# A 384-byte pad ahead of the SBUF tiles, and weight loads whose reads take four rows at once

## The chip, the cores and the metric

The kernel runs on one core of one Trainium2 chip. The metric is the device time of one execution in microseconds (us). Only that core is given work. "Before" is the kernel as it was, "changed" is the kernel with the change.

## The reference

One decode step of an attention layer, gated by a small MLP. Only the sizes matter here: the K and V caches are 268 MB of the 279 MB that are read, and they are read once.

```python
B, Sq, D = 4, 1, 448
Hq, Hkv, Sk, Dh = 16, 8, 8192, 256        # K and V: 4*8 heads of 8192 x 256 bf16 = 4 MiB each
xn = _layernorm(x)
q = (xn @ wq)                              # wq 448 x 4096
scores = einsum(q, k) * Dh ** -0.5         # softmax over 8192 keys
s = (softmax(scores) @ v) @ wo             # wo 4096 x 448
g = _silu(_B_ref(xn, w1, w2, w3, w4))      # _B_ref at S = 1: xn + gelu(layernorm(xn) @ w3) @ w4, w3 448 x 1792, w4 1792 x 448
return x + s * g
```

## The kernel before

All large loads are issued by SP on one queue, in this order: wq, w3, w4, K head 0, K head 1, most of wo, and then in turn K head h and V head h-2. Two buffers hold K, two hold V. The MLP weights lie in the V buffers until V needs them. A partition gets one contiguous row: 32768 B of K or V, 1792 B of wo per query head, 12544 B of w3, 6272 B of w4 (twice).

```python
kn = sb("kn", [P, 2, NCH, DH], BF16)            # first tile of all: byte 16512 of a partition
vb = sb("vb", [P, 2, NCH, DH], BF16)
kT = sb("kT", [P, RING, TB * P], BF16)
wo_sb = sb("wo_sb", [P, HQ, NHALF, D], BF16)
# ... cut
def prog_sp(sp):
    # ... cut: wq -> vb[1]
    sp.dma_start(vflat[0][:, 0:DK * FH], B_w3...).then_inc(S["dw3"], 16)
    sp.dma_start(w4_sb..., B_w4...).then_inc(S["dw4"], 16)

    def load_k(h):
        b, g = where(h)
        if h >= 2:
            sp.wait_ge(S["v_k"], h - 1)          # all of head h-2 has been transposed
        sp.dma_start(kn_dst(h), A_k_cache[b, g]...).then_inc(S["dk%d" % (h % 2)], 16)
    # ... cut: load_v, which waits for v_v in the same way; the last V head comes in four pieces
    load_k(0)
    load_k(1)
    load_wo(NLATE, HQ, "dwo")                    # 12 heads of wo, the early load
    for h in range(2, NH):
        load_k(h)
        load_v(h - 2)
    load_v(NH - 2)
    load_v(NH - 1)
    for i, hs in enumerate(LATE):                # 4 heads of wo, the late load
        load_wo(hs[0], hs[-1] + 1, "dwl%d" % i)
```

PE first computes q and the MLP, then runs warm-up matmuls, then goes through the heads. DVE counts `v_k` up when a head's last group has been copied out.

```python
# PE
for i in range(NWARM):                           # NWARM = 14
    pe.matmul(psv[0:PVW, 0:QW], pT[:, 0, 0:PVW], wq_sb[:, 0, 0:QW], start=True, stop=True)
def f_t(h, j):                                   # group j of 16: transposes of K
    if j == 0:
        take(pe, "dk%d" % (h % 2), 16)
# DVE
for j in range(NGR):
    if j in D_GROUPS:
        evac(v, h, j)                            # waits for the transposes of group j
    # ... cut
v.sem_inc(S["v_k"], 1)
```

Of the kernel before, what the change touches and what calls it, by code (L numbers as in the profile page):

```python
# [1 line left out]

# [8 lines left out]
BF16 = dt.bfloat16  # L11

P = 128
# [19 lines left out]
def bass_recurrent_scan__gqa_block_cached__mixer_s_mlp__decode_kernel(  # L33
# [16 lines left out]
    HQ = HD // DH  # L50
# [3 lines left out]
    NHF = 2  # L54
    DK = D * NHF // P
    assert D * NHF == DK * P and DK % 2 == 1 and D == DK * (P // 2)
    HDH, FH = HD // NHF, F // NHF
    NFK = FH // P
# [30 lines left out]
    LATE = ((0, 1), (2,), (3,))  # L89
    NLATE = sum(len(g) for g in LATE)  # L90
    NWARM = 14
    QW = HDH // NQD
    assert QW <= 512 and QW % P == 0 and NQC == NQD * (QW // P)

# [7 lines left out]
    with ExitStack() as es:  # L102
        def sb(name, shape, dty):
            return es.enter_context(nc.sbuf_tensor(name, shape, dty))

        kn = sb("kn", [P, 2, NCH, DH], BF16)
        vb = sb("vb", [P, 2, NCH, DH], BF16)
        kT = sb("kT", [P, RING, TB * P], BF16)
        wo_sb = sb("wo_sb", [P, HQ, NHALF, D], BF16)
# [46 lines left out]
        S = {n: es.enter_context(nc.semaphore(n)) for n in (  # L156
            ["dx", "dwq", "dw3", "dw4", "dwo", "dk0", "dk1", "dv0", "dv1", "dout"]
            + ["dvl%d" % i for i in range(NPIECE)] + ["dwl%d" % i for i in range(len(LATE))]
            + ["p_td", "p_ta", "p_sc", "p_m1", "p_m2", "p_m3", "p_tr", "p_ou", "p_pv", "p_x", "p_q", "p_h", "p_h2", "p_o"]
            + ["v_ev", "a_ev", "v_rmax", "v_diag", "v_neg", "v_ot", "a_exp", "g_q", "g_c",  # L160
               "v_s", "v_a", "v_qb", "p_qt", "v_h2", "p_hs", "v_k", "v_v", "v_po", "v_o", "g_o", "g_p", "g_f", "v_xT", "v_qT", "v_hT", "v_c", "v_w", "a_c", "v_out"])}


        vflat = [vb[:, i].rearrange("p c d -> p (c d)") for i in range(2)]
        wq_sb = vflat[1][:, 0:DK * HDH].rearrange("p (j n) -> p j n", j=DK)
        w3_sb = vflat[0][:, 0:DK * FH].rearrange("p (j n) -> p j n", j=DK)
        w4_sb = vflat[0][:, DK * FH:DK * FH + NF * D].rearrange("p (a k n) -> p a k n", a=NHF,
                                                                k=NFK)
# [16 lines left out]
        def store(eng, i):  # L185
            eng.dma_start(out2d[:, i * DQ:(i + 1) * DQ], out_b[i * PQ:i * PQ + Bn, :]
                          ).then_inc(S["dout"], 16)

        def prog_sp(sp):
            sp.dma_start(vflat[1][:, 0:DK * HDH],  # L190
                         A_wq.rearrange("d (t n) -> (d t) n", t=NHF).rearrange(
                             "(p j) n -> p (j n)", j=DK)).then_inc(S["dwq"], 16)
            sp.dma_start(vflat[0][:, 0:DK * FH],
                         B_w3.rearrange("d (t n) -> (d t) n", t=NHF).rearrange(
                             "(p j) n -> p (j n)", j=DK)).then_inc(S["dw3"], 16)
            sp.dma_start(w4_sb.rearrange("p a k n -> p a (k n)"),
                         B_w4.rearrange("(a p k) n -> p a (k n)", a=NHF, k=NFK)
                         ).then_inc(S["dw4"], 16)

            def load_k(h):  # L200
                b, g = where(h)
                if h >= 2:
                    sp.wait_ge(S["v_k"], h - 1)
                sp.dma_start(kn_dst(h), A_k_cache[b, g].rearrange("(p c) d -> p (c d)", p=P)
                             ).then_inc(S["dk%d" % (h % 2)], 16)

            def load_v(h):
                b, g = where(h)
                src = A_v_cache[b, g].rearrange("(p c) d -> p c d", p=P)
                if h < NH - 1:  # L210
                    sp.wait_ge(S["v_v"], h + 1)
                    sp.dma_start(vflat[h % 2], src.rearrange("p c d -> p (c d)")
                                 ).then_inc(S["dv%d" % (h % 2)], 16)
                else:

                    sp.wait_ge(S["v_k"], h)
                    for i in range(NPIECE):
                        lo, hi = PIECES[i], PIECES[i + 1]
                        sp.dma_start(
                            kn[:, 1 - h % 2, lo:hi, :].rearrange("p c d -> p (c d)"),  # L220
                            src[:, lo:hi, :].rearrange("p c d -> p (c d)")
                        ).then_inc(S["dvl%d" % i], 16)

            load_k(0)
            load_k(1)
            wo_src = A_wo.rearrange("(h p c) n -> p h (c n)", p=P, c=NHALF)

            def load_wo(lo, hi, sem):
                sp.dma_start(wo_sb[:, lo:hi].rearrange("p h c n -> p h (c n)"),
                             wo_src[:, lo:hi]).then_inc(S[sem], 16)  # L230

            load_wo(NLATE, HQ, "dwo")
            for h in range(2, NH):
# [4 lines that stand above are left out]
            for i, hs in enumerate(LATE):  # L238
                load_wo(hs[0], hs[-1] + 1, "dwl%d" % i)
            sp.wait_ge(S["v_out"], 1)  # L240
            store(sp, 0)
            take(sp, "dout", 16 * NDG)

        def take(eng, name, n=1):
            eng.wait_ge(S[name], n).then_inc(S[name], -n)  # L245
# [285 lines left out]
        def prog_pe(pe, xn_mark, xn2_mark):  # L531
            pe.wait_ge(S["g_c"], NPI)
            for k, (src, mark) in enumerate(((xn_b, xn_mark), (xn2_b, xn2_mark))):
                pe.wait_ge(S["v_c"], mark)
                for j in range(DK):
                    ins = pe.transpose(xT_ps[:, k, j, :],  # L536
                                       src[:, j].rearrange("b m t -> b (m t)"),
                                       ident_b[0:Bn, 0:Bn])
# [5 lines left out]
            for j in range(DK):  # L544
                for i in range(NQD):
                    ins = pe.matmul(q_ps[i * PQ:i * PQ + NHF * Bn, 0:QW],
                                    xnT[:, j].rearrange("p a b -> p (a b)"),
                                    wq_sb[:, j, i * QW:(i + 1) * QW],
                                    start=(j == 0), stop=(j == DK - 1))
# [4 lines left out]
            for k in range(NFK):  # L554
                for j in range(DK):
                    ins = pe.matmul(h_ps[:, k * NHF * Bn:(k + 1) * NHF * Bn], w3v[:, j, k, :],
                                    xn2T[:, j], start=(j == 0), stop=(j == DK - 1))
# [3 lines left out]
                ins = pe.transpose(qt_ps[:, m * P:(m + 1) * P], q_b[:, m * P:(m + 1) * P],  # L561
                                   ident_b[:, :])
            ins.then_inc(S["p_qt"], 1)
            take(pe, "dw4", 16)
            take(pe, "v_hT")
            for k in range(NFK):
                for a in range(NHF):
# [94 lines left out]
            h = NH - 1  # L662
# [39 lines left out]

            def finish():
                f_bc(h)
                take(pe, "dwo", 16)
                pe.wait_ge(S["g_f"], 1)
                f_ou(range(NLATE, HQ - 3 * REP))
                take(pe, "v_po")
                f_warm(4)
                take(pe, "a_exp")  # L710
                pe.matmul(psm[:, P + REP:P + 2 * REP], ones_f[:, :], rowsum[:, h % 2, :],
                          start=True, stop=True)
                f_tr(ot_dst, REP).then_inc(S["p_m3"], 1)
                f_warm(2)
                take(pe, "dv%d" % ((h - 1) % 2), 16)
                f_pv(h - 1, 0, NCH)
                take(pe, "v_ot")
                f_ou(range(HQ - 3 * REP, HQ - 2 * REP))
                f_warm(2)
                take(pe, "v_po")  # L720
                f_tr(lambda dh: ot_dst(dh, 1), REP, 1).then_inc(S["p_tr"], 1)
                f_warm(3)
                take(pe, "dvl0", 16)
                pb = PIECES[NPIECE - ND]
                f_pv(h, 0, PIECES[1], pb, vl)
                take(pe, "v_ot")
                f_ou(range(HQ - 2 * REP, HQ - REP)).then_inc(S["p_ou"], 1)
                f_warm(3)
                for i in range(1, NPIECE - ND):
                    take(pe, "dvl%d" % i, 16)  # L730
                    f_pv(h, PIECES[i], PIECES[i + 1], pb, vl)
                take(pe, "v_a")
                for i in range(NDG):
                    pe.matmul(o_ps[i * PQ:(i + 1) * PQ, 0:DQ], selb[:, :],
                              ou_f[:, i * DQ:(i + 1) * DQ], start=True, stop=False)
                f_direct(NPIECE - ND)
                take(pe, "v_po")
                for dh in range(NHALF):
                    for i in range(CP):
                        pe.matmul(ol_ps[:, dh * PVW:(dh + 1) * PVW],  # L740
                                  po[:, 0, i * DH + dh:(i + 1) * DH:NHALF], sel[:, i, :],
                                  start=False, stop=False)
                f_direct(NPIECE - 1).then_inc(S["p_pv"], 1)
                take(pe, "dwl0", 16)
                f_o(LATE[0])
                take(pe, "v_ot")
                f_o(range(HQ - REP, HQ))
                for i in range(1, len(LATE)):
                    take(pe, "dwl%d" % i, 16)
                    ins = f_o(LATE[i], i == len(LATE) - 1)  # L750
                ins.then_inc(S["p_o"], 1)
# [61 lines left out]
```

## Time and profile before

| before | |
|---|---|
| median of 5 runs | 657.46 us (657.27 to 658.13) |
| span in the profile | 656.9 us |
| DMA rate, 60 to 620 us | 432 GB/s, mean DMA share 1.00 |
| PE busy, same stretch | 484.5 of 560 us |

The first lines are from the page of the kernel before: span, busy time of engines, the mean busy share of the 16 DMA engines in 40 slices (in tenths), the queue's packets with their share of the 16 engines' span, and DMA issues with the median us from issue to landing.

```profile
span 656.9 us, 22864 instructions
...
PE 556.3 (85%) x9937; PEld 476.3 (73%) x9937; DVE 276.5 (42%) x589; ACT 256.0 (39%) x364; POOL 13.4 (2%) x77
...
DMA  8999999999999999999999999999999999999996
...
q1 hardware_dynamic: 12328, 278.99, 99.2%
...
kn<-in_A_k_cache_dram SPq DMA_DIRECT2D x32, 4096.0 KB, 25.7
vb<-in_A_v_cache_dram SPq DMA_DIRECT2D x31, 4096.0 KB, 31.3
...
wo_sb<-in_A_wo_dram SPq DMA_DIRECT2D x1, 2688.0 KB, 44.3
```

The DMA engines are busy in all slices. PE, the busiest compute engine, stands still for 15% of the span. The table of stretches of the kernel before says the same of the middle, and shows that the stretch with the early wo load (36 to 44 us) moves fewer bytes. Its columns are the stretch, its length, busy time of each engine (with instructions), the granted PE clock, the DMA share and GB/s. The rate of a stretch of a few us is coarse, because a packet of 32 KB takes over a microsecond (1213 to 1222 ns, below).

```profile
core 0: us, PE busy (x) PEld busy (x) DVE busy (x) ACT busy (x) POOL busy (x), PEclk, DMA share, GB/s
36.00:44.00 8.00, 8.00 (x174) 7.20 (x170) 3.81 (x8) 4.12 (x5) 0.00 (x0) 1.00 0.95 361
44.00:47.00 3.00, 2.95 (x50) 1.68 (x44) 0.93 (x4) 0.00 (x0) 0.17 (x1) 1.00 1.22 480
47.00:50.00 3.00, 2.00 (x35) 1.86 (x36) 1.81 (x4) 1.41 (x2) 0.01 (x1) 1.00 0.97 415
60.00:620.00 560.00, 484.50 (x8812) 421.48 (x8810) 233.01 (x470) 223.90 (x320) 9.21 (x57) 0.89 1.00 432
```

The timeline of the end shows what follows the last data: 24 matmuls and the first of two DVE steps.

```profile
651.61 2.41 PE L687 MATMUL pst<-wo_sb,OT 128*32 128x224 bf16 x24 [0.50 <-PEq L245]
654.06 0.38 DVE L526 TENSOR_TENSOR res<-pst,sg 64x224 f32<-64x224 f32 x1 [2.61 <-PE pst L687]
```

The trace also has a record of every DMA packet (start, duration, size), from which I work out means below. K and V packets of 32768 B took 1213 to 1222 ns, mean 1217.2, between 100 and 600 us. wo rows of 1792 B took 74 ns at least and 78.4 on average in the early load.

### The profile page before, as it was taken

The numbers are of one execution on the slowest core, as the hardware profiler recorded it, in microseconds if no ns is written. First come the engines' busy times: TensorE is split into PE (matmuls) and PEld (weight loads), VectorE is DVE, ScalarE is ACT, GpSimd is POOL, SyncE is SP. The second block draws the span as 40 slices with busy tenths as digits, with TensorE's granted clock in tenths as the row PEclk, the third lists the DMA queues.
The fourth block names the chain that finished last, engine by engine and source line by source line (L and its number), as shares of the span: only waits on it lengthen the run. The fifth ranks groups of instructions, "written<-read, shape, count | busy, mean of one in ns | idle before, by whom it ended". The sixth has DMA issues, their size and how long they took to land. (4 is left out here: it accounts for less than half of the span.)

```text
span 656.9 us, 22864 instructions
## 1 busy us (share of the span) xinstructions
PE 556.3 (85%) x9937; PEld 476.3 (73%) x9937; DVE 276.5 (42%) x589; ACT 256.0 (39%) x364; POOL 13.4 (2%) x77
## 2 busy tenths in 40 slices
PE   1899997988888988888897888898888889888897
PEld 0487886876766887667787766798767678766775
DVE  7353554443443444434443443444334443433442
ACT  4144544442433443323444333444333344433340
POOL 2000000000000000000000000000000000000000
PEclk9698999887899878889987888988878987887998
DMA  8999999999999999999999999999999999999996
GB/s 360 440 413 425 434 427 437 425 439 427 437 427 435 429 435 431 431 435 427 437 429 433 429 433 429 433 429 433 429 435 431 433 431 435 429 433 433 429 425 256
DMA packets 12353, 279.13 MB, mean 425 GB/s; under 512 B 1204, under 2 KB 3256, under 8 KB 3768
## 3 DMA queue, kind: packets, MB, share of 16 engines
q1 hardware_dynamic: 12328, 278.99, 99.2%
q8 instruction: 7, 0.11, 0.1%
q14 instruction: 2, 0.02, 0.0%
q10 hardware_dynamic: 16, 0.01, 0.0%
HBM read 278.99 MB, written 0.00 MB: 425 GB/s over the span
## 5 line engine op out<-in xcount | busy, mean ns | idle before, releaser
L588 PE MATMUL pst<-ident_b,kn 128*128 128x128 bf16 x4096 | 347.3, 239 | 78.6 <-PEq L245 76.3
L295 ACT ACTIVATE kT<-pst 128x1024 bf16<-128x1024 bf16 x224 | 229.3, 1024 | 360.6 <-ACTq L245 359.5
L588 PEld LDWEIGHTS pst<-ident_b,kn 128*128 128x128 bf16 x4096 | 275.4, 108 | 84.3 <-issue 83.8
L293 DVE COPY kT<-pst 128x1024 bf16<-128x1024 bf16 x288 | 197.5, 691 | 263.7 <-DVEq L245 263.7
L600 PE MATMUL psc<-qc,kT 128*128 128x2 bf16 x4096 | 178.7, 165 | 0.0
L600 PEld LDWEIGHTS psc<-qc,kT 128*128 128x128 bf16 x4096 | 157.7, 98 | 28.5 <-issue 28.3
L639 PE MATMUL psv<-vb,pT 128*4 128x512 bf16 x1056 | 86.4, 378 | 0.3 <-issue 0.3
L618 PE MATMUL psm<-sel,po 128*128 128x2 f32 x272 | 36.8, 257 | 0.5 <-PEq L245 0.5
L618 PEld LDWEIGHTS psm<-sel,po 128*128 128x128 f32 x272 | 34.8, 197 | 0.9 <-issue 0.9
L639 PEld LDWEIGHTS psv<-vb,pT 128*4 128x4 bf16 x1056 | 22.3, 82 | 15.3 <-issue 0.8
L452 DVE TENSOR_REDUCE rmax<-psc 128x2 f32<-128x128 f32 x32 | 9.3, 292 | 48.8 <-DVEq L245 48.8
L470 DVE COPY po<-psv 128x512 f32<-128x512 f32 x34 | 23.5, 692 | 3.0 <-DVEq L245 2.3
L457 DVE TENSOR_REDUCE gmax<-psm 2x1 f32<-2x128 f32 x32 | 8.9, 279 | 34.7 <-DVEq L245 34.7
L317 ACT ACTIVATE pT<-psc,negb 128x64 bf16<-128x64 f32 x66 | 20.6, 331 | 5.4 <-ACTq L245 5.4
L612 PEld LDWEIGHTS psm<-diag,ones_f 2*128 2x128 f32 x66 | 14.1, 263 | 6.4 <-issue 5.4
L280 POOL COPY qc<-qT 128x4 bf16<-128x4 bf16 x32 | 5.9, 186 | 585.8 <-DVEq L469 568.6
L612 PE MATMUL psm<-diag,ones_f 2*128 2x2 f32 x66 | 16.8, 321 | 1.1 <-PEq L245 0.9
L317 ACT ACTIVATION_READ_ACCUMULATOR pT<-psc,negb 128x1 f32 x66 | 13.6, 206 | 0.0
L608 PEld LDWEIGHTS psm<-ident_f,rmax 128*2 128x2 f32 x32 | 2.6, 80 | 14.0 <-issue 14.0
L536 PE MATMUL pst<-ident_b,xn_b 4*128 4x4 bf16 x14 | 0.6, 161 | 13.6 <-DVE xn_b L365 8.9
L630 PE MATMUL psm<-rowsum,ones_f 128*128 128x2 f32 x64 | 11.6, 251 | 0.0
L536 PEld LDWEIGHTS pst<-ident_b,xn_b 4*128 4x128 bf16 x14 | 0.5, 100 | 13.6 <-issue 8.9
(101 smaller groups left out, 122.4 us busy)
## 6 DMA issues: line engine op xcount, KB each, us to landing
kn<-in_A_k_cache_dram SPq DMA_DIRECT2D x32, 4096.0 KB, 25.7
vb<-in_A_v_cache_dram SPq DMA_DIRECT2D x31, 4096.0 KB, 31.3
vb<-in_A_wq_dram SPq DMA_DIRECT2D x1, 3584.0 KB, 11.7
vb<-in_B_w_dram SPq DMA_DIRECT2D x2, 1568.0 KB, 16.6
wo_sb<-in_A_wo_dram SPq DMA_DIRECT2D x1, 2688.0 KB, 44.3
kn<-in_A_v_cache_dram SPq DMA_DIRECT2D x1, 2048.0 KB, 25.2
kn<-in_A_v_cache_dram SPq DMA_DIRECT2D x1, 1024.0 KB, 27.3
kn<-in_A_v_cache_dram SPq DMA_DIRECT2D x2, 512.0 KB, 28.5
```

The costliest lines, as they stand in the source:

```text
L293: engine.tensor_copy(dst, src).then_inc(S["v_ev"], 1)
L295: engine.activation(dst, src, ACT.Copy).then_inc(S["a_ev"], 1)
L317: ins = act.activation(pv_p[:, :, hh], sc[:, :, hh], ACT.Exp, bias=negb[:, s, hh:hh + 1], scale=SCALE, accum_out=rowsum[:, s, hh:hh + 1])
L452: v.tensor_reduce(rmax[:, :], psc[h % 2][:, 0:NCH * REP].rearrange("p (k h) -> p h k", h=REP), AX.X, ALU.max).then_inc(S["v_rmax"], 1)
L457: v.tensor_reduce(gmax[:, :], psm[0:REP, 0:P], AX.X, ALU.max).then_inc(S["v_s"], 1)
L470: v.tensor_copy(po[:, slot], psv[:, 0:CP * DH]).then_inc(S["v_po"], 1)
L588: ins = pe.transpose(dst[:, t * P:(t + 1) * P], kn[:, h % 2, GC * j + kl, half * P:(half + 1) * P], ident_b[:, :])
L600: ins = pe.matmul(psc[h % 2][:, kk * REP:(kk + 1) * REP], kT[:, j % RING, t * P:(t + 1) * P], qc[:, h % 2, half, :], start=(half == 0), st ...
L612: pe.matmul(psm[:, P:P + REP], ones_f[0:REP, :], diag[:, :], start=True, stop=True).then_inc(S["p_m2"], 1)
L618: ins = pe.matmul(dst(dh)[:, 0:width], po[:, slot, i * DH + dh:(i + 1) * DH:NHALF], sel[:, i, 0:width], start=(i == 0), stop=(i == CP - 1))
L630: pe.matmul(psm[:, P + REP:P + 2 * REP], ones_f[:, :], rowsum[:, h % 2, :], start=True, stop=True)
L639: ins = pe.matmul(psv[o:o + CP * REP, 0:CP * DH], pT[:, h % 2, kk * REP:(kk + CP) * REP], src[:, kk:kk + CP, :].rearrange("p c d -> p (c d)"),
```

## The change

The intent: rows that start on an aligned address in SBUF, and fewer, longer reads for the weights whose rows are short. `load_rows` builds the ordinary DMA of 128 rows and replaces its source pattern by 32 rows of four times the length. The destination stays 128 rows, one per partition. Each head of wo and each half of w4 becomes a DMA of its own, so wo takes 16 DMAs instead of 4.

```diff
+    ROW_PAD = 192
+        align = sb("align", [P, ROW_PAD], BF16)
         kn = sb("kn", [P, 2, NCH, DH], BF16)
 ...
+        def load_rows(eng, dst, src, rows, sem):
+            with nc.discard():
+                made = eng.dma_start(dst, src).ins
+            ap, = made.ins
+            n = ap.ap[0][1] * ap.ap[1][1]
 ...
+            pat = [[n // rows, rows], [1, n // rows]]
+            wide = bass.AP(ap.bass_ap.tensor, ap.bass_ap.offset, pat)
+            eng.add_instruction(copy.replace(
+                made, name=nc.get_next_instruction_name(), ant_dge_precooked=False,
+                ins=(copy.replace(ap, ap=pat, bass_ap=wide),))).then_inc(S[sem], 16)
 ...  (w3: one load_rows; w4: one load_rows for each half)
             def load_wo(lo, hi, sem):
-                sp.dma_start(wo_sb[:, lo:hi].rearrange("p h c n -> p h (c n)"),
-                             wo_src[:, lo:hi]).then_inc(S[sem], 16)
+                for hq in range(lo, hi):
+                    load_rows(sp, wo_sb[:, hq].rearrange("p c n -> p (c n)"), wo_src[:, hq],
+                              32, sem)
 ...
-            take(pe, "dw4", 16)
+            take(pe, "dw4", 16 * NHF)
-                take(pe, "dwo", 16)
+                take(pe, "dwo", 16 * (HQ - NLATE))
-                take(pe, "dwl0", 16)
+                take(pe, "dwl0", 16 * len(LATE[0]))
```

More of the change, by code (lines that the diff above doesn't have):

```diff
@@ L1 @@
+import copy
 from contextlib import ExitStack
@@ L187, in store @@
                           ).then_inc(S["dout"], 16)
+        def load_rows(eng, dst, src, rows, sem):
[3 more added lines that the diff above has]
+            n = ap.ap[0][1] * ap.ap[1][1]
+            assert len(ap.ap) == 2 and ap.ap[0] == (ap.ap[1][1], P) and ap.ap[1][0] == 1
+            assert rows % 32 == 0 and P % rows == 0
+            pat = [[n // rows, rows], [1, n // rows]]
[3 more added lines that the diff above has]
+                ins=(copy.replace(ap, ap=pat, bass_ap=wide),))).then_inc(S[sem], 16)
         def prog_sp(sp):
@@ L192, in prog_sp @@
                              "(p j) n -> p (j n)", j=DK)).then_inc(S["dwq"], 16)
-            sp.dma_start(vflat[0][:, 0:DK * FH],
-                         B_w3.rearrange("d (t n) -> (d t) n", t=NHF).rearrange(
-                             "(p j) n -> p (j n)", j=DK)).then_inc(S["dw3"], 16)
-            sp.dma_start(w4_sb.rearrange("p a k n -> p a (k n)"),
-                         B_w4.rearrange("(a p k) n -> p a (k n)", a=NHF, k=NFK)
-                         ).then_inc(S["dw4"], 16)
+            load_rows(sp, vflat[0][:, 0:DK * FH],
+                      B_w3.rearrange("d (t n) -> (d t) n", t=NHF).rearrange(
+                          "(p j) n -> p (j n)", j=DK), 32, "dw3")
+            for i in range(NHF):
+                load_rows(sp, w4_sb[:, i].rearrange("p k n -> p (k n)"),
+                          B_w4.rearrange("(a p k) n -> p a (k n)", a=NHF, k=NFK)[:, i],
+                          32, "dw4")
             def load_k(h):
```

## The prediction

> **What bounds the kernel now.** The DMA engines. In the table of stretches, 100 to 620 us has a mean DMA share of 1.00 at 432 GB/s (431.6 from the packet records), while PE is busy 86%, DVE and ACT about 40%. The queue table puts 99.2% of 16 engines' span on one queue. Only the first 2 us and the last 5 us (24 matmuls of L687, two DVE steps, the store) are not transfer. K and V come as 504 packets of 32 KB per engine, one row each. The list of SP's waits shows that issue runs well ahead (DMAs land 25 to 31 us after issue), so time is the sum of packet times.
>
> **What a packet costs.** Packet records, smallest or median durations: 32768 B 1213 ns (mean 1217), 12544 B 469, 6272 B 239, 1792 B 74 (mean 78 in the early wo load), 4 B 9. [...] The compiled program puts the first tile at byte 16512 of a partition[...]. [...]
>
> **What the change does.** The pad of 384 B moves kn, vb, wo_sb to multiples of 512. Wide reads turn runs of four rows (wo 1792 B, w4 6272 B[...]) into one read of 7168 or 25088 B; the writes remain one per partition. wo becomes 16 DMAs instead of 4, w4 two instead of one: 13 more DMAs, each about 0.4 us of SP issue (hidden, issued some 30 us ahead) and one 9 ns completion packet per engine.
>
> **Worth, on the critical path (estimates from those durations).**
> - [...]
> - [...]
> - wo early, 96 packets per engine, 78.4 to about 69: 0.9 us. (In the stretches 36 to 44 us the rate is about 360 GB/s.)
> - w3, w4: 0.1 us.
> - wo late, 32 packets: 0.2 us at the DMA, about 0.1 visible, since PE's own chain before L687 (ready 651.45) is as late as the data (651.5).
> - 13 completions: -0.1 us.
>
> Sum 3.6 us, discounted a little for the assumption: predicted 654.0 us, 80% range 652.6 to 656.9. Chances: faster by over 2%: 0.01; within 2%: 0.97; slower by over 2%: 0.02.
>
> **What would show it.** Pad: K/V packets fall from 1213-1218 to 1208-1213 ns, and 100 to 620 us moves at 433 to 434 GB/s. Wide reads: wo packets of 66 to 70 ns per row[...]; 36 to 44 us near 400 GB/s. Spans of all engines' work unchanged; more PE wait on K saved, none added.
>
> **What would make it wrong.** If the 8 ns is inherent per packet, the pad is worth nothing and only about 1 us remains (656.5). [...] If the write side alone limits, wide reads give nothing beyond the pad. If [...]the twelve small DMAs starve the queue, the early load slows by a microsecond or more.

The sum came to 3.6 us. The four terms that still stand make 1.0 us of it (0.9 + 0.1 + 0.1 - 0.1). The two terms of the pad, 2.6 us together, are cut, because what they took off a row was in no trace. The assumption for which the sum was discounted is that the place where a written tile starts counts at all. The packets of 1208-1213 ns and the 433 to 434 GB/s expected from the pad rest on the same cut terms; they were my estimate. The 8 ns of the last paragraph can be had from the packet records of the kernel before: a straight line through the smallest durations of 32768 B (1213 ns) and 1792 B (74 ns) has 36.8 ns per 1000 B and 8.1 ns besides, and over that slope the packets of 12544 B (469 ns) and 6272 B (239 ns) carry 7.8 and 8.4 ns. That is an estimate. The 69 ns of the early wo load follow from the same line: 1792 B make 65.9 of the 78.4 ns, and a quarter of the other 12.5 is 3.1.

## More of the kernel before

The timeline of SP in the kernel before (start, duration, line, transfer) shows when the queue gets new work. The early wo load and everything ahead of it are issued by 4 us. The load of K head 2 comes only at 42.68 us.

```profile
3.28 0.49 SPq L229 DMA_DIRECT2D wo_sb<-in_A_wo_dram  x1
42.68 0.33 SPq L204 DMA_DIRECT2D kn<-in_A_k_cache_dram  x1
46.79 0.33 SPq L212 DMA_DIRECT2D vb<-in_A_v_cache_dram  x1
```

The DMA share of the stretch from 44 to 47 us reads 1.22, so its 480 GB/s is no real rate.

## The result, and the profile after

A ratio here is the mean time of one kernel's fast runs over that of the other's of the same rounds, so it is not quite the ratio of the medians quoted. All runs were fast runs, with granted clocks between 0.88 and 0.91 where one is on record.

| | median us | lowest to highest | runs | ratio to before, 95% |
|---|---|---|---|---|
| before | 657.46 | 657.27 to 658.13 | 5 | |
| changed | 656.24 | 654.86 to 657.24 | 5 | 0.9971 (0.9959 to 0.9984) |

The change is clear of noise and small: 0.29%, or 1.9 us by the ratio. Two things stand out. The median lies 2.2 us above the predicted 654.0, and the changed kernel's runs lie 2.4 us apart where those of the kernel before lie 0.9 apart. The second is a weak sign by itself: in the later rounds the kernel before was run 11 times beside the experiments, and there its runs lay 1.0 to 2.9 us apart, in three of four sets because of a single late run (660.24, 659.57, 659.50). The profile was taken of one of the fastest runs (654.93 us). Here are the same lines of its page.

```profile
span 653.1 us, 22877 instructions
...
PE 552.2 (85%) x9937; PEld 472.4 (72%) x9937; DVE 275.5 (42%) x589; ACT 255.9 (39%) x364; POOL 13.4 (2%) x77
...
DMA  9999999999999999999999999999999999999997
...
q1 hardware_dynamic: 10712, 278.99, 99.3%
...
kn<-in_A_k_cache_dram SPq DMA_DIRECT2D x32, 4096.0 KB, 24.9
vb<-in_A_v_cache_dram SPq DMA_DIRECT2D x31, 4096.0 KB, 30.4
...
wo_sb<-in_A_wo_dram SPq DMA_DIRECT2D x16, 224.0 KB, 34.1
```

Packets went from 12328 to 10712, since a read of four rows is one record (384 records of 7168 B in the early wo load, where the kernel before has 1536 of 1792 B). The rate over the span rose, and wo now comes as 16 DMAs. The table of stretches of the changed kernel:

```profile
core 0: us, PE busy (x) PEld busy (x) DVE busy (x) ACT busy (x) POOL busy (x), PEclk, DMA share, GB/s
36.00:44.00 8.00, 6.88 (x147) 6.46 (x144) 3.38 (x8) 4.08 (x4) 0.00 (x0) 1.00 0.94 389
44.00:47.00 3.00, 3.00 (x55) 1.48 (x56) 0.63 (x2) 0.00 (x0) 0.00 (x0) 1.00 1.12 406
47.00:50.00 3.00, 2.95 (x53) 2.69 (x52) 2.45 (x6) 1.55 (x2) 0.19 (x1) 1.00 0.94 404
60.00:620.00 560.00, 482.68 (x8836) 419.54 (x8833) 233.79 (x471) 224.35 (x321) 9.21 (x57) 0.89 1.00 433
```

The middle gained one GB/s as rounded there. From the packet records, 60 to 620 us, it is 431.65 before and 433.01 after, 0.31%. The stretch of the early wo load rose from 361 to 389 GB/s. But the 6 us behind it fell, from 480 and 415 to 406 and 404. Averaged over the three stretches (weighted by 8, 3 and 3 us), the rate is 398 GB/s before and 396 after: the gain of the load is gone by 50 us. SP's timeline of the changed kernel shows the load of K head 2 at 43.71 us.

```profile
4.71 14.33 SPq L196 DMA_DIRECT2D wo_sb<-in_A_wo_dram  x12
43.71 0.33 SPq L223 DMA_DIRECT2D kn<-in_A_k_cache_dram  x1
47.82 0.33 SPq L231 DMA_DIRECT2D vb<-in_A_v_cache_dram  x1
```

By the packet records, the DMA engines are then nearly through with the early wo load. The first packet of K head 2 starts at 44.67 us, and twelve packets of 32 KB that start between 43.5 and 50 us take 1340 to 2413 ns instead of 1213.

The end of the changed kernel, beside that of the kernel before:

```profile
649.09 1.44 PE L707 MATMUL pst<-wo_sb,OT 128*32 128x224 bf16 x24 [0.36 <-PEq L265]
...
650.56 0.38 DVE L546 TENSOR_TENSOR res<-pst,sg 64x224 f32<-64x224 f32 x1 [1.51 <-PE pst L707]
```

The 24 matmuls took 1.44 us instead of 2.41, because the granted clock was 1.00 there and 0.53 in the profile of before. Over the 14 profiles the time from the last wo packet to the end lies between 3.38 and 4.75 us. It may hang on the clock granted there and on PE's own chain, which is not shown, so I do not credit it to the change. Of the 3.8 us between the two profiled spans, 2.2 us come from the last V packet of head 30 (639.89 to 637.70 us, the last of the 32 KB packets), 0.2 us from the pieces of V and the late wo behind it, and 1.4 us from this tail.

### The profile page after: what moved, and what is told of

Same layout as the page of the kernel before. It is cut to its first block, busy times and chain, and to the rows that moved or that the text cites. A ratio compares the mean times of both kernels' runs of the same rounds, so it can differ in the third digit from the quotient of the medians.

```text
span 653.1 us, 22877 instructions
## 1 busy us (share of the span) xinstructions
PE 552.2 (85%) x9937; PEld 472.4 (72%) x9937; DVE 275.5 (42%) x589; ACT 255.9 (39%) x364; POOL 13.4 (2%) x77
## 3 DMA queue, kind: packets, MB, share of 16 engines
q1 hardware_dynamic: 10712, 278.99, 99.3%
## 5 line engine op out<-in xcount | busy, mean ns | idle before, releaser
L608 PEld LDWEIGHTS pst<-ident_b,kn 128*128 128x128 bf16 x4096 | 272.5, 107 | 84.0 <-issue 83.4
L638 PE MATMUL psm<-sel,po 128*128 128x2 f32 x272 | 36.8, 257 | 0.5 <-PEq L265 0.5
```

The source lines that it names most:

```text
L608: ins = pe.transpose(dst[:, t * P:(t + 1) * P], kn[:, h % 2, GC * j + kl, half * P:(half + 1) * P], ident_b[:, :])
L638: ins = pe.matmul(dst(dh)[:, 0:width], po[:, slot, i * DH + dh:(i + 1) * DH:NHALF], sel[:, i, 0:width], start=(i == 0), stop=(i == CP - 1))
```

## The experiments

My theory after the first reading: the pad does nearly all, by way of the K and V packets. The wide reads do shorten the wo loads, but the load of K head 2 waits for PE to finish head 0, and with the early wo load gone sooner the queues run dry before it arrives. I call that the gap. The rivals: the wide reads carry the gain; or the many small DMAs and not the gap cost time.

Each kernel ran beside the kernel before on the same chip, but e1 to e4 ran on one chip, e5 to e11 on a second and e12 on a third. The kernel before had medians of 657.41 to 657.87 us in these sets. So only the ratios compare across sets, and a difference of under 0.5 us between medians of two sets means nothing.

| | kernel | median us | lowest to highest | ratio to before, 95% |
|---|---|---|---|---|
| e1 | pad alone | 655.16 | 654.78 to 655.51 | 0.9954 (0.9942 to 0.9966) |
| e2 | wide reads alone | 657.86 | 657.40 to 658.00 | 0.9995 (0.9983 to 1.0008) |
| e3 | pad of 128 B alone | 655.18 | 655.09 to 655.54 | 0.9956 (0.9943 to 0.9968) |
| e4 | changed, again | 655.66 | 654.78 to 657.70 | 0.9968 (0.9950 to 0.9985) |
| e5 | pad, wide early wo only | 655.39 | 654.74 to 657.77 | 0.9973 (0.9961 to 0.9986) |
| e6 | pad, wide reads except early wo | 655.34 | 654.57 to 656.02 | 0.9965 (0.9952 to 0.9978) |
| e7 | changed, 9 warm-ups | 656.57 | 654.98 to 657.69 | 0.9981 (0.9969 to 0.9993) |
| e8 | pad alone, 9 warm-ups | 654.88 | 654.61 to 656.23 | 0.9961 (0.9948 to 0.9974) |
| e9 | changed, K head 2 in halves | 654.88 | 654.41 to 655.57 | 0.9959 (0.9947 to 0.9971) |
| e10 | pad alone, K head 2 in halves | 655.15 | 654.84 to 656.01 | 0.9964 (0.9952 to 0.9975) |
| e11 | pad of 32 B alone | 657.77 | 657.34 to 658.75 | 1.0005 (0.9989 to 1.0021) |
| e12 | pad alone, 24 warm-ups | 662.13 | 659.63 to 665.23 | 1.0068 (1.0043 to 1.0094) |

From the packet records of the one profile of each: the mean K/V packet between 100 and 600 us; the mean ns of a wo row in the early load; when K head 2 was issued; how many us later its first packet started; how many 32 KB packets that start between 43.5 and 50 us were slow (over 1300 ns; in e9 and e10 16 KB packets over 700); and the end of the last 32 KB packet, the slowest DMA engine's.

| | K/V ns | wo row ns | K2 issued | to first packet | slow | last 32 KB packet |
|---|---|---|---|---|---|---|
| before | 1217.2 | 78.4 | 42.68 | 2.14 | 1 | 639.89 |
| changed | 1213.2 | 69.0 | 43.71 | 0.96 | 12 | 637.70 |
| e1 | 1213.1 | 74.3 | 42.69 | 1.94 | 2 | 637.40 |
| e2 | 1217.2 | 74.6 | 42.81 | 2.06 | 2 | 639.92 |
| e3 | 1213.2 | 74.3 | 42.52 | 1.95 | 3 | 637.41 |
| e4 | 1213.2 | 69.0 | 42.83 | 1.40 | 24 | 638.30 |
| e5 | 1213.1 | 69.0 | 42.67 | 1.68 | 14 | 637.13 |
| e6 | 1213.1 | 74.6 | 43.35 | 1.40 | 10 | 637.82 |
| e7 | 1213.2 | 69.0 | 42.95 | 1.43 | 24 | 639.12 |
| e8 | 1213.1 | 74.3 | 43.91 | 0.96 | 15 | 638.01 |
| e9 | 1213.2 | 69.0 | 36.06, 42.19 | 8.24 | 1 | 636.93 |
| e10 | 1213.1 | 74.3 | 36.28, 42.14 | 8.24 | 1 | 637.18 |
| e11 | 1217.1 | 78.7 | 42.67 | 2.34 | 1 | 639.45 |
| e12 | 1214.0 | 74.3 | 46.87 | 0.96 | 16 | 643.84 |

The next table is the best witness of where time goes. It counts the bytes of the load queue (q1) that have arrived by a given time, takes those of e1 away, and divides by 433 GB/s: how many us a kernel's stream is ahead of e1 (plus) or behind it (minus), as a mean of the 16 engines. It rests on one profile of each kernel; the kernels with the same loads agree within 0.2 us wherever no gap parts them.

| ahead of e1, us | at 36 | at 44 | at 50 | at 100 | at 300 | at 635 |
|---|---|---|---|---|---|---|
| before | -0.02 | -0.23 | -0.39 | -0.57 | -1.24 | -2.39 |
| e2 wide alone | +0.12 | -0.14 | -0.27 | -0.44 | -1.11 | -2.30 |
| e11 pad 32 B | +0.04 | -0.23 | -0.38 | -0.55 | -1.21 | -2.33 |
| e3 pad 128 B | +0.07 | +0.06 | +0.05 | +0.04 | +0.03 | +0.02 |
| changed | +0.10 | +0.26 | -0.37 | -0.49 | -0.49 | -0.53 |
| e4 changed again | +0.11 | +0.27 | -0.31 | -0.45 | -0.45 | -0.49 |
| e7 changed, 9 warm-ups | +0.19 | +0.35 | -0.45 | -0.66 | -0.65 | -0.69 |
| e5 early wide | +0.08 | +0.25 | +0.06 | -0.10 | -0.10 | -0.14 |
| e6 rest wide | +0.05 | +0.01 | -0.26 | -0.40 | -0.40 | -0.39 |
| e8 pad, 9 warm-ups | +0.04 | +0.03 | -0.58 | -0.59 | -0.58 | -0.59 |
| e9 changed, halves | +0.21 | +0.38 | +0.40 | +0.37 | +0.37 | +0.33 |
| e10 pad, halves | +0.09 | +0.08 | +0.07 | +0.05 | +0.05 | +0.04 |
| e12 pad, 24 warm-ups | -0.02 | -0.06 | -3.39 | -3.45 | -3.50 | -4.44 |

Read along a row. The kernels whose tiles start off a multiple of 256 B (before, e2, e11) fall behind at a steady pace to the end (before: -0.57 us at 100, -1.24 at 300, -2.39 at 635). The changed kernel is ahead by a quarter of a microsecond at 44 us, loses 0.6 us in the 6 us that follow, and then stays level with the pad alone.

In every profile one slow packet of this stretch starts just as a 16 KB packet of the instruction queue ends; in most it takes about 1680 ns. In e1, e2 and e3 one or two more are slow, 1354 to 1512 ns, among the first packets of K head 2: these kernels are close to the gap too.

### e1: the pad alone

```diff
 (to the kernel before)
+    ROW_PAD = 192
+        align = sb("align", [P, ROW_PAD], BF16)
```

> The pad without the wide reads. Theory A (the pad takes the slow packets of K and V away, the wide reads only shorten the early and late wo loads): K/V packets all 1213 ns as in the changed kernel (before: 1213 to 1222, mean 1217), 60 to 620 us at 433.0 GB/s against 431.6, the last V packet lands about 2.0 us earlier than in the kernel before, and wo rows of 1792 B cost about 74 ns each instead of 78. Time about 2 to 2.5 us under the kernel before, 655.1, with runs that differ by well under 1 us, because the first queue gap at 44 us that the changed kernel shows is smaller with narrow reads. Rival B (the wide reads bring most, by fewer descriptors): within 1 us of the kernel before, 431.6 GB/s.

Measured: ratio 0.9954, which is 3.0 us, the fastest median of the first four. The K/V packets are all 1213 ns. A wo row costs 74.3 ns instead of 78.4 with no wide read. The runs lie 0.7 us apart. The stretches of e1 show no dip behind the early wo load:

```profile
36.00:44.00 8.00, 8.00 (x172) 7.21 (x171) 3.81 (x8) 4.13 (x5) 0.00 (x0) 1.00 0.96 378
44.00:47.00 3.00, 2.95 (x50) 1.67 (x44) 0.93 (x4) 0.00 (x0) 0.17 (x1) 1.00 1.16 479
47.00:50.00 3.00, 2.55 (x49) 2.41 (x50) 2.07 (x5) 1.96 (x3) 0.02 (x1) 1.00 1.07 459
60.00:620.00 560.00, 483.74 (x8795) 420.72 (x8793) 232.42 (x470) 223.91 (x319) 9.29 (x57) 0.89 1.00 433
```

So the pad alone gives at least as much as the whole change. That it gives more is likely but not shown by the times, since the intervals overlap (0.9942 to 0.9966, and 0.9959 to 0.9984 or, in e4, 0.9950 to 0.9985).

### e2: the wide reads alone

```diff
 (to the changed kernel)
-    ROW_PAD = 192
-        align = sb("align", [P, ROW_PAD], BF16)
```

> The wide reads without the pad. Theory A: K/V packets keep 1213 to 1222 ns, mean 1217; the early wo load ends about 0.8 us earlier than before (47.0 us), but the load of the third K head, issued at about 43 to 44 us when the first head has been worked through, finds the queues nearly empty, so most of that is lost again: time within 0.8 us of before, spread over 1 us between runs. Rival B: 1.5 to 2 us faster than before.

Measured: ratio 0.9995, nothing. But the reason that I gave was wrong: the profile has no gap, and the early load's last packet ended only 0.07 us sooner (46.95 against 47.02), not 0.8. A wide read of four rows took 298.5 ns, or 74.6 per row, against 69.0 with the pad. So without the pad wide reads take only 3.8 ns off a row, and the stream is 0.1 us ahead of that of before all along (-2.30 against -2.39 at the end), from w3 and w4. The spread was 0.6 us.

### e3: 128 B instead of 384

```diff
-    ROW_PAD = 192
+    ROW_PAD = 64
```

> The pad alone with 128 B instead of 384: the tiles start at a multiple of 256 B but not of 512. If a write must start on a 256 B boundary to be fast, K/V packets are 1213 ns and the time is that of the pad of 384 B, within 0.5 us. If 512 B is what counts, they stay at a mean of 1217 and the time is that of the kernel before.

Measured: as the pad of 384 B, in time (655.18 and 655.16) and in packets. Tiles on a multiple of 256 B were enough here (1213.2 ns for a K/V packet, 1213.1 in e1). 512 B gave nothing more.

### e4: the changed kernel again

> The changed kernel once more, for its spread: before, five runs lay within 0.9 us, the changed kernel's within 2.4. If the spread comes from the gap that its queues have at 44 us and from where the throttled clock falls in the last 24 matmuls, its runs again lie 1.5 us or more apart, between 654.8 and 657.3; if the first five were chance, they lie within 1 us.

Measured: 654.78 to 657.70 over six runs, so the spread is the kernel's own. Its profile has a gap with 24 slow packets, its stream falls from 0.27 us ahead to 0.31 behind, and the last 32 KB packet came 0.9 us later than with the pad alone. Against e1 on the same chip the changed kernel is 0.5 us slower by the median and 0.8 us by the mean, with a standard error of 0.5 us. The last 32 KB packet and the table above are the better evidence.

### e5 and e6: wide reads in the early wo load only, and everywhere else

```diff
 (e5, to the changed kernel: w3, w4 and the late wo as before)
+                if lo < NLATE:
+                    sp.dma_start(wo_sb[:, lo:hi]..., wo_src[:, lo:hi]).then_inc(S[sem], 16)
+                    return
 (e6, to the changed kernel: the early wo as before)
+                if lo >= NLATE:
+                    sp.dma_start(wo_sb[:, lo:hi]..., wo_src[:, lo:hi]).then_inc(S[sem], 16)
+                    return
```

> Pad, and wide reads for the early wo load only (w3, w4 and the late wo as before). Theory: the early load ends some 0.5 us sooner than with the pad alone, so the queues run dry before the load of the third K head comes (issued at 42.5 to 43.7 us), and every engine's first K packets then take 1300 to 2400 ns instead of 1213: the gap of the changed kernel is there, median 655.2 to 656.2, runs 1.5 us or more apart. Rival (the many small DMAs at the start or the end are to blame, not the gap): like the pad alone, 654.8 to 655.5.

> Pad, and wide reads for w3, w4 and the late wo, but the early wo load as one DMA of narrow reads. Theory: no gap at 44 us, runs within 0.8 us of each other, and a median of 654.8 to 655.1, up to 0.3 us under the pad alone (the late wo lands some 0.2 us sooner, w3 and w4 0.1 us). Rival: as slow and as spread as the changed kernel.

Measured: e5 has the median and the spread expected (3.0 us), though the median lies in the rival's range as well. Its profile fell on the fastest run, 654.74, with 14 slow packets and a loss of only 0.35 us (from +0.25 to -0.10). e6 missed: its median is above the range expected, the spread is 1.5 us, and its profile has a gap without a wide read in the early load. K head 2 was issued at 43.35 us there, 0.7 us later than in e1. So the gap goes with the margin between two times, the end of the early load and the issue of K head 2, and the second moves by a microsecond between profiles. The table gives the margin: where 1.9 us or more lie between issue and first packet (before, e1, e2, e3, e11) there are one to three slow packets, with 1.4 to 1.7 us (e4 to e7) there are 10 to 24, and in changed, e8 and later e12 it was 0.96 us each time, the least seen, with 12, 15 and 16.

### e7 and e8: nine warm-up matmuls

```diff
-    NWARM = 14
+    NWARM = 9
```

> The changed kernel with 9 instead of 14 warm-up matmuls, which hold PE until 31.0 us although the first K head has landed at 29.4. Theory: PE starts the first head 1.5 us sooner, the third K head's load is issued at about 41.5 us, while the queues still hold the early wo load, the gap at 44 us vanishes, and only then the wide reads pay: median 654.2 to 654.8, runs within 0.8 us. If the gap is not what costs, the time stays at 655.7 with a spread of over 1.5 us.

> Control: the pad alone with 9 warm-up matmuls. There is no gap to close with narrow reads, so theory says no change against the pad alone: 654.8 to 655.5. If it gains as much as the changed kernel does, the warm-up itself was a cost and not the gap.

e7 missed. The median of e8 fell in its range, but its profile has the gap that it was to be without. The idea was to close the gap by an earlier issue of K head 2, but the issue did not come earlier: 42.95 us in e7, 43.91 in e8. PE did start head 0 at 29.70 us in e7 instead of 30.90, but lost 1.12 us on the way. In e8 it started at 30.75, which is 1.23 us after a 16 KB packet of the instruction queue ended. The same 1.22 or 1.23 us stand between such a packet and the start of head 0 in e2, e5, e10 and e11. But in e8 the last piece of K head 0 landed at that moment too (29.51 us), so this is a hint and no proof. So neither run tests what it was made for. They serve in another way: e8 has narrow reads only and a gap with 15 slow packets, which costs 0.6 us (+0.03 to -0.58), and its runs spread over 1.6 us instead of 0.7.

The loss on the way is in the changed kernel's profile as well. In its timeline of PE, the bracket gives the idle time ahead of an instruction and what ended it ("issue": nothing that the profile shows):

```profile
40.30 0.61 PE L608 MATMUL pst<-ident_b,kn 128*128 128x128 bf16 x8
42.02 0.35 PE L620 MATMUL psc<-qc,kT 128*128 128x2 bf16 x8 [1.12 <-issue]
```

PE stood still for 1.12 us in the middle of head 0, with its data there. That is about the microsecond by which K head 2 is issued later than in the kernel before (43.71 against 42.68). A 16 KB packet of the instruction queue ran from 39.74 to 40.70 us, just ahead of it. The other traces have the same pattern. In e4, e5, e6, e7 and twice in e12 PE also stood still in head 0, for 0.54 to 1.38 us. All seven stops ended 1.26 to 1.44 us after a 16 KB packet of the instruction queue did. A late instruction load may be the cause. That is my reading of the times; no run here varied it, so it is not shown.

### e9 and e10: K head 2 in two halves

The K buffer is released in halves for this one load. The first half is issued when DVE has copied out group 8 of head 0. SP passes the completion on to PE's semaphore.

```diff
 (e9, to the changed kernel; e10, to e1)
                 if h == 2:
+                    for i, (sem, n) in enumerate((("v_kh", 1), ("v_k", h - 1))):
+                        sp.wait_ge(S[sem], n)
+                        lo, hi = i * NCH // 2, (i + 1) * NCH // 2
+                        sp.dma_start(kn[:, h % 2, lo:hi, :]..., ksrc[:, lo:hi, :]...).then_inc(S["dkh"], 16)
+                    return
 ...  (after load_k(2) and load_v(0))
+                    sp.wait_ge(S["dkh"], 32)
+                    sp.sem_inc(S["dk0"], 16)
 ...  (DVE, in each head)
+                        if j == 8:
+                            v.sem_inc(S["v_kh"], 1)
```

> The changed kernel, with the load of the third K head in two halves: the first is issued when half of its buffer is free (about 37 us), so that the queues can't run dry at 44 us. Theory (the wide reads pay 0.5 us in the early load and that is lost to the gap, which also makes the spread): no stretch under 370 GB/s between 44 and 47 us, no K packet group of 1300 to 2400 ns there, last V packet near 637.0 us (pad alone 637.4, changed 637.7), median 654.3 to 654.8, runs within 0.8 us. Rival (the gap is not the cause): median 655.7, spread 1.5 us or more.

> Control: the pad alone with the same two halves. The gap of the pad alone is absent in most runs, so at most 0.3 us: 654.8 to 655.2. If it gains as much as the changed kernel, the wide reads are worth nothing even without the gap; the difference between this kernel and the one with wide reads and halves is what the wide reads are worth, 0.5 us by theory.

Measured: e9 has a median of 654.88 us and a spread of 1.2 us, against 655.66 and 2.9 of the changed kernel in e4. SP's timeline of e9 shows the first half issued at 36.06 us (the two halves are merged into one line), and its stretches show the dip filled:

```profile
4.24 14.63 SPq L196 DMA_DIRECT2D wo_sb<-in_A_wo_dram  x12
36.06 6.47 SPq L227 DMA_DIRECT2D kn<-in_A_k_cache_dram  x2
46.30 0.33 SPq L241 DMA_DIRECT2D vb<-in_A_v_cache_dram  x1
```

```profile
36.00:44.00 8.00, 7.73 (x160) 6.62 (x160) 3.64 (x7) 3.41 (x4) 0.00 (x0) 1.00 0.94 386
44.00:47.00 3.00, 2.95 (x49) 1.97 (x46) 1.43 (x5) 0.44 (x1) 0.19 (x1) 1.00 1.10 457
47.00:50.00 3.00, 2.16 (x49) 2.04 (x47) 1.69 (x5) 1.63 (x3) 0.00 (x0) 1.00 1.01 431
```

There is no slow packet but the usual one, and the lead of 0.38 us at 44 us is kept to the end (+0.33). The last 32 KB packet ends at 636.93 us, the earliest of all, 0.8 us ahead of the changed kernel. e10, with narrow reads, gained nothing over e1 (ratios 0.9964 and 0.9954), as the theory has it. The median expected for e9 (654.3 to 654.8) was just missed, and so was the spread (0.8 us).

Between e9 and e10 stands what the wide reads are worth without a gap: 0.3 us by the median, 0.25 us at the last 32 KB packet, 0.3 us in the stream (+0.33 against +0.04). The intervals of the ratios overlap (0.9959 and 0.9964), so that size is not settled.

### e11: a pad of 32 B

```diff
-    ROW_PAD = 192
+    ROW_PAD = 8
```

In the compiled program the pad of 16 B takes 32 B, and the first tile lies at byte 16544, 160 B past a multiple of 256.

> The pad alone at 32 B: tiles start 160 B past a multiple of 256 B, and no longer on a multiple of 64. If only the 256 B boundary matters, K/V packets keep a mean of 1217 ns and the time is that of the kernel before, within 0.5 us. If lesser boundaries matter too, packets are longer than before and the time is over 658.5.

Measured: the packets and the time of the kernel before. Of the four addresses tried, the two on a multiple of 256 were fast (mean K/V packet 1213.1 and 1213.2 ns), and being 160 past it cost what being 128 past it cost (1217.1 and 1217.2 ns).

So the cost did not grow with the distance past the multiple: 4.0 ns over e1 at 160 B, 4.1 at 128 B. Nor is it a fixed cost of each row that starts off such a multiple. In the three kernels without a useful pad (before, e2, e11), 228 of the 229 K packets that start by 24 us, leaving out the few over 1300 ns, took 1213 or 1214 ns, like aligned ones. A row of w3, which lies 128 B off before the change, took 469 ns both before and in e1. Only later do the long rows become slower (mean 1217.1 or 1217.2 ns from 100 to 600 us). What turns the cost on stays open.

### e12: the gap on purpose

```diff
 (to e1)
-    NWARM = 14
+    NWARM = 24
```

> The gap made on purpose, without any wide read: the pad alone with 24 instead of 14 warm-up matmuls, so that the first head ends about 2 us later and the load of the third K head is issued near 44.5 us instead of 42.7, when the early wo load (over at 44.5 to 46.4 us on the 16 engines) is almost through. Theory: a gap at 45 to 47 us, the first K packets at 1300 to 2400 ns, the last V packet 1 to 2 us later than the pad alone (637.4), median 656.0 to 657.3 against 655.2. Rival (the spread and loss of the changed kernel come from the wide descriptors or the number of DMAs, not from the gap): 654.8 to 655.5 as the pad alone, since PE is not what bounds the rest.

Measured: K head 2 was issued at 46.87 us, later than meant because PE stood still twice in head 0 (0.62 and 1.38 us), and the median is 662.13 us, 7 us over the pad alone. The stretches of e12 show the hole where e1 has none:

```profile
36.00:44.00 8.00, 7.18 (x153) 6.84 (x149) 3.56 (x7) 5.13 (x10) 0.00 (x0) 1.00 0.96 378
44.00:47.00 3.00, 1.81 (x44) 1.65 (x44) 0.98 (x3) 0.95 (x1) 0.00 (x0) 0.98 0.44 167
47.00:50.00 3.00, 3.00 (x46) 1.19 (x46) 0.69 (x2) 0.00 (x0) 0.00 (x0) 0.50 0.92 311
```

There is no wide read in this kernel. From 44 to 47 us the queues moved 167 GB/s, from 47 to 50 us 311 GB/s with 16 slow packets. PE then had half its clock (0.50), and V head 0 was issued late too (52.94 us against 46.80 in e1). The stream fell 3.3 us behind by 50 us and never made it up, and another microsecond went between 300 and 635 us: two packets of 2044 and 2436 ns at 332 us mark the place. There the instruction queue was busy: it carried 17 packets of 16 KB in e12 and 7 in every other profile. The slowest engine lost more than the mean: the last 32 KB packet came 6.4 us later than in e1. The loss is larger than expected, but of the kind expected: a gap at this place goes into the time. How much of the 7 us and of the spread (5.6 us) comes from the gap, and how much from the extra instruction loads, this run cannot tell.

## Why the prediction was right and where it failed

The measured median lies inside the stated range, near its upper end. Point by point:

- **What bounds the kernel.** "The DMA engines": right. In e12 the stream lost 3.3 us where the queues ran empty (DMA share 0.44 from 44 to 47 us) and never won it back.
- **Pad: 2.6 us of the sum.** Right in effect. The mean packet fell by 4.1 ns, which is 2.1 us over 504 packets. All of the pad, other rows included, is worth 2.4 us in the stream at 635 us (before against e1) and 3.0 us in e1's time by the ratio; the tail may hold the rest. The address of the tile that is written made the difference here: 1213.1 and 1213.2 ns on a multiple of 256 B (e1, e3), 1217.2 and 1217.1 ns 128 or 160 B past one (before, e11). The assumption that this address counts held. That the size came out near is in part luck, as the next point says.
- **How the pad works.** Wrong. I took the 8 ns over the bytes in the smallest packets (the estimate beside the prediction) for a cost of which the pad would save the larger part, and expected 1208 to 1213 ns; no trace showed that split. The smallest K/V packet between 100 and 600 us stayed at 1213, and a wo row at 74 ns. Aligned packets carry the 8 ns too (1213 ns in the changed kernel, as before). What the pad took away is the part above the floor: 55% of K/V packets between 100 and 600 us took 1218 ns or more, now 0.1%. A cost of every row that grows with the distance past a multiple of 256 B does not explain this: a row 160 B off cost no more than one 128 B off (4.0 and 4.1 ns), and the first K rows cost nothing extra (1213 or 1214 ns, e11). That a fall of up to 5 ns was predicted and 4.1 measured does not confirm the way it was predicted.
- **wo early: 0.9 us, from 78.4 to about 69 per row.** Right as a packet time: it is 69.0. But 4.1 of the 9.4 ns are the pad's. Of the other 5.3 ns (0.5 us over 96 rows) part is not real, since records of narrow packets overlap more: from 36 to 44 us their durations sum to 1.035 of the 16 engines' time in e1, and to 1.015 in the changed kernel. In the stream the wide early load is worth 0.2 us (e9, from +0.21 at 36 us to +0.40 at 50), and in the changed kernel none of it reached the end.
- **w3, w4, the late wo and the completions.** Of the size stated in the packet records (w3 and w4 0.14 us, a completion 9 ns), too small to see in the time.
- **The step that failed**: "issue runs well ahead (DMAs land 25 to 31 us after issue), so time is the sum of packet times." The 25 to 31 us are medians over all loads. At one place issue is not far ahead of the stream: K head 2 is the first load that must wait for compute, and in the kernel before it was issued only 2.1 us ahead of its first packet. Make the load in front of it a few tenths shorter, and let PE be late by up to a microsecond, and the queues run low. So of the term "wo early, 0.9 us" only the part that the pad brings was paid. The rest was lost in a gap that cost 0.6 to 0.8 us in three profiles of the same wide loads (changed, e4, e7); in e9 the gap is closed and the lead is kept, and in e6, e8 and e12 there is a gap without wide early reads. With it came a spread of 2.4 to 3.0 us between runs (changed, e4, e5, e7), but that the gap makes it is not shown: the profiles of the changed kernel and of e5 have the gap and fell on fast runs (654.93 and 654.74).

Four things stay open: whether late instruction loads are what stops PE in head 0, why packets just after the gap are slow, what turns on the cost of a start off a multiple of 256 B, and what makes the spread; only one run of each kernel has a trace, so the slow runs of the changed kernel were not looked into one by one.

The best version by the numbers is e9: 654.88 us, 0.8 us under the changed kernel of e4 by the median (0.6 us by the ratios, which allow for the other chip), with under half its spread. The intervals of the two ratios overlap (0.9947 to 0.9971, and 0.9950 to 0.9985), so this is not shown beyond doubt. The pad of 128 B alone, e3, is as good within 0.3 us, at one line of code.

## What to carry to other kernels

Look up at which byte the first tile starts: this kernel, which streams rows of 32 KB with a DMA share of 1.00 from 60 to 620 us, gained 0.44% (e3) from 128 B of padding. Before a load is made shorter in a stream that runs at its limit, look for the first transfer behind it that waits for compute, and subtract: does the queue still hold work when that transfer is issued, on the fastest DMA engine and in the slowest run? Here K head 2 came with one to three slow packets where it was issued 1.9 us or more ahead of its first packet, and with 10 to 24 where it was 0.96 to 1.7 us. The median times from issue to landing (25.7 and 31.3 us before) hid that one place. When runs of a new version scatter more than those of the old, look whether a margin has been used up.
